# Fused sparse attention and mixer: start-up order, transposes of the first batch, place of the strided work, and the last accumulation step

## The chip, the cores and the metric

The kernel runs on one core of a Trainium2 chip. The metric is the device time of one execution in microseconds (us): the median of three runs, and, for the analysis, one profiled execution with its trace.

The core has five engines with a queue each, worked off in order: TensorE (PE, with PEld for its weight loads), VectorE (DVE), ScalarE (ACT), GpSimd (POOL) and SyncE (SP). SP, ACT and POOL also start DMA transfers; a DMA that has to wait holds up what stands behind it in the same queue.

## The reference

There are 8 batches of 8 heads, 576 positions and head size 64. Heads 0 to 3 attend to the last 32 positions ("local"), heads 4 to 7 to the positions of the same residue modulo 32 ("strided"). The attention output, 576 x 512 for a batch, then goes through a mixer:

```
scores = q @ k.T / 8, masked (local or strided), softmax, @ v  -> x
h = x^T @ U @ V            (U: 576 x 32, V: 32 x 576)
u = x + h^T
out = u + relu(u @ w_ch1) @ w_ch2      (512 -> 2048 -> 512)
```

## The kernel before

**The blocks.** The two large products are made block by block. A block n has four row tiles of 128 positions of one batch; a ninth block holds the last 64 positions of all batches. A block has 16 steps fc: `gemm1` (12 matmuls, L668) makes 128 hidden columns, ACT and DVE split the result into a high and a low part `gh`, `gl` (L673, L674), and one step later `gemm2` (12 matmuls, L686) adds them into four accumulators, each 128 x 512 in PSUM, held in two tiles of two. `finish` (L693) adds the accumulators to x on DVE, one row tile after the other, and stores them. Operands are split in high and low parts because the fast number format is not exact; `split` (L659, L660) does this for u at the end of a block, from `raw`, which 32 small DMAs fill from transposed tiles `bt` (`transposes`).

**The start-up.** `first_attention` makes the attention of batches 0 and 1 in eight head pairs, four a batch, in the order strided, strided, local, local. The text calls them P1 to P8 in that order (P1 to P4 are batch 0). A pair loads k and q together (`load_qk`), then v (`load_v`); PE adds the mask into PSUM as a matmul with the bf16 identity `ident_b` (L338) and then the scores (L357); DVE takes maximum and difference (L367, L368), ACT the exponential (L372); PE transposes the result with the f32 identity `ident` (L379), ACT copies it out (L382), PE multiplies by v (L397), DVE divides (L408 to L415). For batch 0 `quarter` follows: it transposes the pair's part of x with `x_transposed` (L312, a matmul with `ident`), multiplies by U (L286, L288), adds the product with V on top of the transposed x (L295), and splits the sum into a quarter of `uh`, `ul`. The first step of block 0 needs all four quarters. Idle stretches of PE ahead of P1's and P2's scores are filled with `WARM` matmuls on zeros (L336), eight each. The three constants (strided mask, local mask with `ident_b`, and `ident`) are loaded on POOL's queue; everything else comes on SP's queue. `small_weights` converts U (L129 to L132, two copies L144, L145) and then V, in separate steps of the start-up.

**The weights** come as 64-bit words. They are loaded on SP in 23 units and converted on ACT and DVE (L129, L131, L132, L205, L206) during block 0, up to four steps ahead of their use. The buffer `early` also lies in the place of the first large unit.

**The rest of the attention.** In block n the attention of batch n+1 is made in small steps that `advance` hands out by slot (two slots a step, 32 a block): `A_EARLY`, `A_LATE`, `A_TAIL` say from which slot to which slot how many steps. From batch 2 on, the strided heads are made without PE in `strided_heads`: POOL multiplies (L467 scores, L495 values), DVE sums (L445, through `reduced`, which puts a sum behind the last `finish` traced before it). `S0` and `S1` say in which slots, `N_STRIDED` how many steps; for batch 2 it starts in slot 16 of block 0, and its steps run from slot 22 to slot 12 of block 1. When the attention reaches the mark "strided", what is left of the strided steps is issued at once, and then `strided_copies` (L512, L516) moves the result into x on ACT, followed by `mix_t`, `mix_u`, `mix_tail` and `transposes`.

**What sets the order.** The program is traced in the order of the code, and a list scheduler with a time model then fixes each engine's order; `tc.issue_after` adds an edge. So a slot is a priority and, through buffers and edges, sometimes a bound; it is no fixed time.

## Time and profile before

| | us |
|---|---|
| median of three runs | 918.03 |
| lowest, highest | 916.94, 919.47 |
| the profiled execution, its own time | 918.08 |
| span of its trace, first to last instruction | 916.0 |
| PE busy / DVE busy / POOL busy / ACT busy in the span | 893.4 / 548.3 / 339.4 / 253.2 |

The profiled execution is 0.05 us from the median, so sums made on its trace can be compared with the median directly. Busy times have to be read stage by stage: the share of PE in the span is a mean over a start-up, nine blocks and a tail, and an engine with a low share can still be the one that a stage waits for.

### The profile page before, as it was taken

To read this page: it belongs to the slowest core of one execution; us is meant where nothing else is said; L and a number is where in the kernel's file an instruction comes from. 1 tells how busy PE (TensorE), PEld (TensorE's weight loads), DVE (VectorE), ACT (ScalarE), POOL (GpSimd) and SP (SyncE) were. 2 spreads that over 40 slices of the span, in tenths; PEclk is the share of its full clock that TensorE was granted. 3 is DMA by queue.
4 is the path that set the end of the run, shared out by engine and by line. 5 is a ranking of instruction groups with operands and counts; after the bars stand their busy time and mean duration, and the time that the engine had idled before them with its cause. 6 is when DMAs were issued, how large, how long until landed. Compare 5 with 4: busy or idle time off the path is not lost.

```text
span 916.0 us, 16587 instructions
## 1 busy us (share of the span) xinstructions
PE 893.4 (98%) x6862; PEld 714.1 (78%) x6862; DVE 548.3 (60%) x899; ACT 253.2 (28%) x501; POOL 339.4 (37%) x378
## 2 busy tenths in 40 slices
PE   7899989999999999999999999999999999999997
PEld 4677768887888787878887888878787888888885
DVE  4678997856786588738873877477754331122111
ACT  3456422241224122521242123312241211121110
POOL 1232484636563475429450946175620000000000
PEclk9899999999999999999999999999999999999999
DMA  9869313210331015011401050103200230001001
GB/s 355 308 211 357 118 44 116 72 53 3 86 135 42 12 52 183 1 53 31 165 28 53 21 187 28 53 9 124 91 1 3 57 116 23 1 1 47 0 1 47
DMA packets 30843, 75.27 MB, mean 82 GB/s; under 512 B 6464, under 2 KB 14672, under 8 KB 28848
## 3 DMA queue, kind: packets, MB, share of 16 engines
q1 hardware_dynamic: 29360, 71.07, 22.6%
q0 software_dynamic: 1088, 2.62, 0.9%
q8 instruction: 54, 0.88, 0.4%
q10 hardware_dynamic: 320, 0.52, 0.2%
q14 instruction: 21, 0.17, 0.1%
HBM read 54.14 MB, written 11.67 MB: 72 GB/s over the span
## 4 chain that ended last, share of the span: by engine, by line
PE 84%; DVE 4%; DMA 2%; POOL 1%; issue 1%; ACT 1%; SPq 0%; DVEq 0%; POOLq 0%; ACTq 0%
PE acc L686 40%; PE ph L668 39%; PE px L397 1%; DMA w<-in_w_dram 1%; PE px L357 1%; PE px L379 1%; DVE s_st L445 1%; PE px L536 1%; PE px L558 1%; DVE cv L132 1%; DMA st<-in_strided_dram 1%; DVE w L206 1%; DMA od<-x 1%; DVE gl L674 0%; POOL tmp L467 0%
## 5 line engine op out<-in xcount | busy, mean ns | idle before, releaser
L674 DVE SCALAR_TENSOR_TENSOR gl<-ph,gh 128x512 fp32r<-128x512 f32 x144 | 98.5, 685 | 233.7 <-ACT gh L673 232.9
L467 POOL TENSOR_TENSOR tmp<-st 128x576 f32<-128x576 f32 (+6 forms) x162 | 177.0, 1128 | 127.6 <-DMA st<-in_strided_dram 71.7
L668 PE MATMUL ph<-uh,w 128*128 128x512 f32 x648 | 215.4, 391 | 0.0
L673 ACT ACTIVATE gh<-ph 128x512 fp32r<-128x512 f32 x144 | 85.7, 597 | 449.0 <-PE ph L668 424.8
L686 PE MATMUL acc<-w,gh 128*128 128x512 f32 x648 | 196.3, 391 | 0.0
L495 POOL TENSOR_TENSOR tmp<-st,s_st 128x448 f32<-128x448 f32 (+7 forms) x162 | 137.0, 876 | 128.2 <-DVE st L445 51.2
L686 PEld LDWEIGHTS acc<-w,gh 128*128 128x128 f32 x648 | 121.2, 188 | 26.8 <-issue 1.2
L668 PEld LDWEIGHTS ph<-uh,w 128*128 128x128 f32 x648 | 121.7, 188 | 26.0
L445 DVE TENSOR_REDUCE st<-tmp 128x64 f32<-128x64 f32 (+8 forms) x162 | 135.6, 882 | 2.6 <-POOL tmp L495 2.1
L668 PE MATMUL ph<-ul,w 128*128 128x512 f32 x324 | 126.4, 390 | 0.0
L686 PE MATMUL acc<-w,gl 128*128 128x512 f32 x324 | 121.8, 391 | 4.2 <-DVE gl L674 4.2
L445 DVE TENSOR_REDUCE s_st<-tmp 128x9 f32<-128x576 f32 (+6 forms) x162 | 86.4, 561 | 14.0 <-POOL tmp L467 13.4
L686 PEld LDWEIGHTS acc<-w,gl 128*128 128x128 f32 x324 | 60.8, 188 | 18.7 <-DVE gl L674 5.9
L668 PEld LDWEIGHTS ph<-ul,w 128*128 128x128 f32 x324 | 60.8, 188 | 12.5
L512 ACT COPY xg<-st 32x256 f32<-32x256 f32 x96 | 38.8, 404 | 10.7 <-DVE st L445 9.0
L660 DVE TENSOR_TENSOR ul<-raw,uh 128x256 fp32r<-128x256 f32 x64 | 25.4, 432 | 12.9 <-ACT uh L659 12.5
L693 DVE TENSOR_TENSOR xg<-acc,xg 128x512 f32<-128x512 f32 x36 | 22.7, 682 | 17.4 <-PE acc L686 17.4
L659 ACT CAST uh<-raw 128x256 fp32r<-128x256 f32 x64 | 23.2, 404 | 19.5 <-DMA raw<-bt 10.2
L668 PE MATMUL ph<-uh,w0a 128*128 128x512 f32 x72 | 24.1, 391 | 0.0
L668 PE MATMUL ph<-uh,w1a 128*128 128x512 f32 x72 | 23.9, 391 | 0.0
L668 PE MATMUL ph<-uh,w2a 128*128 128x512 f32 x72 | 23.9, 391 | 0.0
L668 PE MATMUL ph<-uh,w6a 128*128 128x512 f32 x72 | 23.8, 392 | 0.0
(266 smaller groups left out, 1231.6 us busy)
## 6 DMA issues: line engine op xcount, KB each, us to landing
w<-in_w_dram SPq DMA_DIRECT2D x9, 1024.0 KB, 13.3
raw<-bt SPq DMA_DIRECT2D x256, 32.0 KB, 1.8
out_dram<-xg SPq DMA_DIRECT2D x32, 256.0 KB, 5.2
v<-in_pairs_dram SPq DMA_DIRECT2D x12, 585.0 KB, 5.1
st<-in_strided_dram SPq DMA_DIRECT2D x6, 1152.0 KB, 5.5
qk<-in_pairs_dram SPq DMA_DIRECT2D x12, 576.0 KB, 6.1
late<-in_pairs_dram SPq DMA_DIRECT2D x8, 585.0 KB, 8.2
late<-in_pairs_dram SPq DMA_DIRECT2D x8, 576.0 KB, 8.1
```

The lines of the kernel that those rows point to most:

```text
L132: nc.vector.scalar_tensor_tensor(out=i, in0=lo_w, scalar=29, in1=i, op0=ALU.logical_shift_right, op1=ALU.bitwise_or)
L445: nc.vector.tensor_reduce(**what)
L467: nc.gpsimd.tensor_tensor(out=tmp[:, 0:n], in0=sk[:, j0:j0 + n], in1=sq[:, i:i + 1].broadcast_to([128, n, D]), op=ALU.mult)
L495: nc.gpsimd.tensor_tensor(out=tv, in0=sv[:, 0:i + 1, d0:d0 + step], in1=s_st[:, i, 0:i + 1].broadcast_to([128, i + 1, step]), op=ALU.mult)
L512: nc.scalar.copy(out=xg[32 * i4:32 * i4 + 32, :, cs], in_=o_st[rows, i4:16:4, :])
L659: nc.scalar.copy(out=hi, in_=raw[:, t, :, :, dc, :])
L660: nc.vector.tensor_tensor(out=lo, in0=raw[:, t, :, :, dc, :], in1=hi.bitcast(F32), op=ALU.subtract)
L668: last = nc.tensor.matmul(ph, w_parts[fc, 0][:, part, 128 * dc:128 * dc + 128], ut[:, dc, :], start=(dc == dcs[0] and i == 0), stop=(dc == ...
L673: marks.setdefault("gh", []).append(nc.scalar.activation(out=gh, in_=ph, func=AF.Relu).ins)
L674: low = nc.vector.scalar_tensor_tensor(out=gl, in0=ph, scalar=0.0, in1=gh.bitcast(F32), op0=ALU.max, op1=ALU.subtract)
L686: last = nc.tensor.matmul(accs[n][s // 2][:, s % 2, :], gt[:, cs], w_parts[fc, 1][:, part, :], start=(fc == 0 and i == 0 and n > 0), stop= ...
L693: last = nc.vector.tensor_tensor(out=ot, in0=accs[n][s // 2][:, s % 2, :], in1=ot, op=ALU.add)
```

## The change

**Start-up.** One DMA on SP, first in that queue, brings the strided mask and `ident_b` together (`mask_first`, in `early`). `ident` follows on SP behind the k and q of P1 and P2, the local mask behind the v of P1. POOL loads none of them. The second group of `WARM` matmuls falls from eight to three. U's conversion stands behind the second exponential, where it stood behind the first copy of transposed probabilities, and in one step with V's.

**Transposes.** `x_transposed` uses TensorE's transpose mode.

**Strided work and attention slots.** For batch 2 the strided work starts in slot 20 (its steps from slot 26) and ends by slot 20 of block 1. The value products go by residue of the chunk index modulo 4, and the ACT copies into x become steps of `strided_heads`, one group behind the sums. The attention steps of blocks 1 to 6 go in two paces, local pairs first and then the mix, with own slots for block 1.

**Last step.** In the last step of the last block the accumulators are completed tile by tile, in order, and the fourth lies in a tile of its own.

```diff
-N_LATE = 47
-N_STRIDED = 66
+N_LOCAL = 20
+N_REST = 16
+N_STRIDED = 74
...
-A_LATE = (2, 26, N_LATE)
+A_LATE = (3, 12, 26)
+A_SECOND = (1, 19, 27)
...
-S0 = {2: 16, **{b: 32 * (b - 1) - 12 for b in range(3, 8)}}
-S1 = (12, 12)
+S0 = {2: 20, **{b: 32 * (b - 1) - 12 for b in range(3, 8)}}
+S1 = (20, 12)
 ORDER0 = (2, 3, 0, 1)
-WARM = {0: 8, 1: 8}
+WARM = {0: 8, 1: 3}
...
-    masks_sb = const.tile([128, 448], BF16, name="masks_sb")
-    mask_l, ident_b = masks_sb[:, 0:320], masks_sb[:, 320:448]
+    mask_l = const.tile([128, 320], BF16, name="mask_l")
...
-    mask_s = early[:, 1600:1760].bitcast(BF16)
+    mask_first = early[:, 1600:1824].bitcast(BF16)
+    mask_s, ident_b = mask_first[:, 0:320], mask_first[:, 320:448]
...
-        with tc.issue_after(marks["PT"][0]), tc.issue_after(marks["less"][1]):
+        with tc.issue_after(marks["exp"][1]), tc.issue_after(marks["less"][1]):
             f = to_f32(words_in, early, 128, 10 * R)
         nc.scalar.copy(out=U_sb.rearrange("p t r -> p (t r)"), in_=f[:, 0:5 * R])
         nc.scalar.copy(out=late[0][:, 1816:1816 + 5 * R], in_=f[:, 5 * R:10 * R])
-        yield
...
                 return nc.tensor.matmul(pu[:, 128 * t:128 * t + n], part, ident[0:n, 0:n], start=t == 0, stop=False,
-                                        skip_group_check=True).ins
+                                        is_transpose=True, skip_group_check=True).ins
...
-        far_dma(out=mask_s, in_=masks[:, 448:768])
-        far_dma(out=masks_sb, in_=masks[:, 0:448])
-        far_dma(out=ident, in_=eye)
-        for first in (heads[0], heads[1], heads[0], heads[2], heads[1], sw, heads[3], heads[2], heads[3]):
+        dma(out=mask_first, in_=masks[:, 0:448])
+        for n, first in enumerate((heads[0], heads[1], heads[0], heads[2], heads[1], sw, heads[3], heads[2], heads[3])):
             next(first)
+            if n == 1:
+                dma(out=ident, in_=eye)
+            if n == 2:
+                dma(out=mask_l, in_=masks[:, 448:768])
...
-            if tick in (1, 2):
+            if tick == 2:
                 next(sw)
...
-            accs[n] = [ps_acc.tile([128, 2, 512], F32, name="acc") for _ in range(2)]
-        for s in range(4):
+            pair = [ps_acc.tile([128, 2, 512], F32, name="acc") for _ in range(2)]
+            accs[n] = [pair[s // 2][:, s % 2, :] for s in range(4)]
+            if n == B:
+                accs[n][3] = psx1()
+        for s in tiles:
...
-        if len(pend) > 1:
+        if len(pend) > 1 and step < len(steps) - 1:
             gemm2(*pend.pop(0))
...
-    while pend:
-        gemm2(*pend.pop(0))
+    gemm2(*pend[0])
+    for s in range(4):
+        with tc.issue_after(marks["acc"][-1]):
+            gemm2(*pend[1], (s,))
     finish(NB - 1)
```

In `strided_heads` the loop over the 18 chunks becomes a loop over the groups (16 and 17; 0, 4, 8, 12; 1, 5, 9, 13; 2, 6, 10, 14; 3, 7, 11, 15); when a group's sums have been traced, the four heads' ACT copies of the group before are traced, with a step after every second head. `strided_copies` is gone, and the attention goes from the mark "strided" to `mix_t`.

## Rows read from the trace of the kernel before

**Rows 1.** The page's first part: busy time of each engine, its share of the span and its instructions.
```profile
PE 893.4 (98%) x6862; PEld 714.1 (78%) x6862; DVE 548.3 (60%) x899; ACT 253.2 (28%) x501; POOL 339.4 (37%) x378
```

**Rows 2.** TensorE's matmuls in order of time in the start-up, merged: start, length, line, operands, count, and in brackets the idle time before and what ended it. The last row is P8's mask.
```profile
8.08 0.68 PE L338 MATMUL acc<-early,masks_sb 128*128 128x320 bf16 x2 [3.23 <-DMA masks_sb<-in_masks_dram]
8.69 1.31 PE L357 MATMUL acc<-late 64*32 64x32 f32 x72
9.94 2.69 PE L336 MATMUL px<-raw 128*128 128x512 bf16 x8
...
13.18 0.86 PE L379 MATMUL acc<-ident,late 128*128 128x128 f32 x5
...
18.94 1.52 PE L312 MATMUL acc<-ident,early 128*128 128x128 f32 x10
...
29.40 2.69 PE L312 MATMUL acc<-ident,early 128*128 128x128 f32 x10
...
34.64 1.24 PE L379 MATMUL acc<-ident,late 128*128 128x128 f32 x5
...
37.82 1.16 PE L312 MATMUL px<-ident,xg 128*128 128x128 f32 x8
...
43.66 1.13 PE L312 MATMUL acc<-ident,xg 128*128 128x128 f32 x8 [1.28 <-DVE xg L411]
...
48.75 0.50 PE L668 MATMUL ph<-uh,w0a 128*128 128x512 f32 x1
...
57.61 0.45 PE L338 MATMUL acc<-masks_sb 128*128 128x320 bf16 x2
```

**Rows 3.** DMA issues by line, with count, size and median us from issue to landing: P1's k and q (the first issue of the first us), P2's (the second), U, and the last stores on ACT's queue.
```profile
late<-in_pairs_dram SPq DMA_DIRECT2D x1, 576.0 KB, 4.1
...
late<-in_pairs_dram SPq DMA_DIRECT2D x1, 576.0 KB, 5.3
...
xg<-in_U_dram SPq DMA_DIRECT2D x1, 320.0 KB, 9.2
...
out_dram<-xg ACTq DMA_DIRECT2D x4, 128.0 KB, 3.4
```

**Rows 4.** SP's queue in order of time: start, length, what is issued, count.
```profile
0.74 2.59 SPq L96 DMA_DIRECT2D late<-in_pairs_dram  x5
3.38 0.49 SPq L96 DMA_DIRECT2D xg<-in_U_dram  x1
...
46.68 0.33 SPq L96 DMA_DIRECT2D w<-in_w_dram  x1
...
227.45 20.14 SPq L96 DMA_DIRECT2D raw<-bt  x32
```

**Rows 5.** Busy time of one slice of one us: start and end, length, busy us of PE, PEld, DVE, ACT, POOL with instruction counts, granted TensorE clock, DMA share, GB/s.
```profile
29.00:30.00 1.00, 1.00 (x33) 0.83 (x16) 0.49 (x1) 0.00 (x0) 0.00 (x0) 0.50 0.99 394
```

**Rows 6.** ScalarE in order of time: the first weight conversion, P3's copy of transposed probabilities, the first large unit's conversion, and the last casts of `split` for block 2.
```profile
19.95 0.67 ACT L129 ACTIVATE cv<-w0a 128x512 f32<-128x512 f32 x1 [0.60 <-DMA w0a<-in_w_dram]
...
24.96 0.63 ACT L382 COPY late<-px 128x576 f32<-128x576 f32 x1
...
77.98 1.15 ACT L129 ACTIVATE cv<-w 128x1024 f32<-128x1024 f32 x1
...
249.17 1.02 ACT L659 CAST uh<-raw 128x256 fp32r<-128x256 f32 x3 [0.62 <-DMA raw<-bt]
```

**Rows 7.** What TensorE waited for from 75 to 130 us and from 130 to 880 us (us in total, times, longest); the first row is of the first stretch, the second the largest of the second.
```profile
PE acc L686 <- DVE gl L674: 3.5, 3, 1.6
...
PE acc L686 <- DVE gl L674: 0.7, 1, 0.7
```

**Rows 8.** VectorE in order of time: one weight subtraction without and one beside POOL's products, and the seventeenth sum of batch 2's scores.
```profile
95.51 1.20 DVE L206 TENSOR_TENSOR w<-cv,w 128x1024 fp32r<-128x1024 f32 x1
...
111.76 2.34 DVE L206 TENSOR_TENSOR w<-cv,w 128x1024 fp32r<-128x1024 f32 x1
...
130.84 0.38 DVE L445 TENSOR_REDUCE s_st<-tmp 128x4 f32<-128x256 f32 x1
```

**Rows 9.** GpSimd in order of time: the gate of batch 2's strided load, and its value products.
```profile
99.52 0.40 POOL L452 COPY st<-w 1x1 f32<-1x1 f32 x1 [16.45 <-ACT w L205]
...
161.87 7.51 POOL L495 TENSOR_TENSOR tmp<-st,s_st 128x320 f32<-128x320 f32 x9 [9.22 <-DVE st L445]
...
187.83 2.29 POOL L495 TENSOR_TENSOR tmp<-st,s_st 128x576 f32<-128x576 f32 x2 [0.85 <-DVE st L445]
```

**Rows 10.** The page's costliest groups: busy us and mean ns of one, then idle time before and its releaser.
```profile
L467 POOL TENSOR_TENSOR tmp<-st 128x576 f32<-128x576 f32 (+6 forms) x162 | 177.0, 1128 | 127.6 <-DMA st<-in_strided_dram 71.7
```

**Rows 11.** The chain that ended last, in order of time, around the first mix of batch 2 and the start of block 2.
```profile
212.02 1.00 PE px L536 x8
...
247.56 5.44 PE acc L686 x24
253.00 5.44 PE ph L668 x24
```

**Rows 12.** All engines in order of time at the end.
```profile
908.68 2.48 DVE L693 TENSOR_TENSOR xg<-acc,xg 128x512 f32<-128x512 f32 x4 [3.21 <-PE acc L686]
...
909.16 0.39 PE L686 MATMUL acc<-w,gl 128*128 128x512 f32 x1
...
909.41 2.74 ACTq L99 DMA_DIRECT2D out_dram<-xg  x4
```

More of the change, by code (lines that the diff above doesn't have):

```diff
@@ new lines, in strided_heads @@
+        done = []
+        for i4 in (4, 0, 1, 2, 3, None):
+            for i in () if i4 is None else range(16, NCH) if i4 == 4 else range(i4, 16, 4):
+                step = D if i < 9 else D // 2
+                for d0 in range(0, D, step):
+                    tmp = att([128, (i + 1) * step], "tmp")
+                    tv = tmp.rearrange("p (j d) -> p j d", d=step)
+                    nc.gpsimd.tensor_tensor(out=tv, in0=sv[:, 0:i + 1, d0:d0 + step],
+                                            in1=s_st[:, i, 0:i + 1].broadcast_to([128, i + 1, step]), op=ALU.mult)
+                    late.append(lambda tv=tv, i=i, d0=d0, step=step: reduced(
+                        out=o_st[:, i, d0:d0 + step], in_=tv.rearrange("p j d -> p d j"), axis=AX.X, op=ALU.add))
+                    flush(1)
+                    yield
+            flush(0)
+            done.append(i4)
+            if len(done) == 1:
+                continue
+            i4 = done[-2]
+            assert len(marks["out"]) == b - 1
+            xg, xt = x_tiles(b)
+            for h in range(4):
+                rows = slice(32 * h, 32 * h + 32)
+                cs = slice(256 + D * h, 256 + D * h + D)
+                if i4 < 4:
+                    nc.scalar.copy(out=xg[32 * i4:32 * i4 + 32, :, cs], in_=o_st[rows, i4:16:4, :])
+                else:
+                    for x in range(2):
+                        nc.scalar.copy(out=xt[tb + 32 * x:tb + 32 * x + 32, cs], in_=o_st[rows, 16 + x, :])
+                if h % 2:
+                    yield
@@ L692, in finish @@
             ot = xgs[n][:, s, :]
[L693 removed]
+            last = nc.vector.tensor_tensor(out=ot, in0=accs[n][s], in1=ot, op=ALU.add)
             if n == B:
```

48 lines of the change are left out of this document (13 added, 35 removed).

## The prediction

> **What bounds the kernel now.** I read the busy times first, then PE in order of time, then what PE waits for. PE is busy 893.4 of 916.0 us [rows 1], so all idle time of PE together is 22.6 us, and only work taken off PE can bring more. The question is where these 22.6 us lie. Of the waits, the largest after the start-up are for `gl`, 3.5 us between 75 and 130 and 0.7 from there to 880 [rows 7]. At the end PE's last matmul ends at 909.16 + 0.39 = 909.55, and the span at 916.0, which is 6.4 us [rows 12]. The rest, some 12 us, lies in the main ahead of the first gemm, which starts at 48.75 [rows 2]. So blocks 0 to 8 are PE-bound, and a gain comes from an earlier first gemm, from the stalls of block 0, or from the tail. What the reader should see in the start-up: PE's first scores stand behind a wait of 3.23 us for a mask [rows 2], and part of it runs at a granted clock of 0.50, which is 1.2 of 2.4 GHz [rows 5].
>
> **The masks.** The first scores are released by `masks_sb` at 8.08, at 8.69 they start [rows 2]. P1's k and q have landed at 0.74 + 4.1 = 4.84 [rows 3, 4]. After the change the mask lies ahead of them in the same queue: one more issue of 2.59 / 5 = 0.52 us [rows 4]. So P1's scores start near 5.4 instead of 8.69, -3.2 us; the bounds are -3.9 (the extra issue hidden) and 0 (the landing in its new queue no earlier than now). `ident` and the local mask come behind the loads of P1 and P2; the transposes that need `ident` come after scores, maximum, difference and exponential, 13.18 - 8.69 = 4.5 us later than the scores [rows 2], and that covers it. Without that cover it would cost the 0.5 us of an issue. They delay every load behind them by up to three issues, 1.5 us, where the queue's issue and not the transfer is the limit.
>
> **The warm matmuls.** Eight take 2.69 us, 0.34 each, at mixed clock [rows 2]; five fewer are -1.7. P2's k and q, the second in the queue, are there at about 1.3 + 5.3 + 0.5 = 7.1 [rows 3, 4], and P1's scores and three warm matmuls end at 5.4 + 1.3 + 1.0 = 7.7, so P2's scores can use all of it. P1's own chain, through DVE and ACT to its transposition, doesn't pass the warm matmuls and wins nothing. Of two chains that alternate on the same engines I count one: -0.8, bounds -1.7 and 0.
>
> **The transposes of x.** L312 now shows 10 matmuls for five tiles, L379, a transposition, five for five [rows 2]. The four quarters cost 1.52, 2.69 (at half clock), 1.16 and 1.13; as transpositions 0.86, 1.24 (L379 at half clock), and four tiles of 0.86 / 5 twice, 0.69. That is -0.66, -1.45, -0.47, -0.44, in sum -3.0. The first three stand among work of PE without a pause before them, so most of this is on its path; before the last PE waits 1.28 for DVE, and the transposition follows in the chain itself [rows 2]. I take -2.2, bounds -3.0 and 0. The Trainium skill (TensorE: Matmul & The Clock Gate, Terms) calls the transpose mode 4 times faster for FP32: by that the four would cost a quarter, and the sum be -4.9. The rows give a factor of 1.6 to 2.2, and I go by the rows.
>
> **U's steps.** U lands at 3.38 + 9.2 = 12.6 [rows 3, 4], which doesn't move. If the first pair is 3 us earlier, U's conversion behind the first copy would stand in ACT's queue before its data are there, and behind it the second exponential; moved behind that exponential it meets data that have landed. The same instructions run, and P1's multiplication by U waits for them: 0, bounds -1 and +1.
>
> **What doesn't move.** The first weights land at 19.95 [rows 6], at the end of a row of loads; the DMA engines are still full at 29 us, with a share of 0.99 [rows 5]. ACT copies P3's transposed probabilities at 24.96 behind the conversions [rows 6]. If ACT keeps that order, the copy can't come earlier than 19.95 plus the conversion itself, two casts and two vector steps of 0.4 to 0.7, an estimate of 2.4 us from the first row's 0.67: 22.4, or -2.6 us. So of the 4.0 us from masks and warm matmuls, 1.4 can be lost here. I take +1.2, bounds 0 and +1.4.
>
> **Start-up, sum:** -3.2 - 0.8 - 2.2 + 1.2 = -5.0; bounds -8.6 and 0 (U's +1 or -1 aside). The pairs of batch 1 and the weight loads behind them start from the same work and move with it, so I take the shift through block 0 undiminished. `early` is now held until P8's mask is in PSUM, as `ident_b` lies in it, and the first large weight unit waits for that: its load was issued at 46.68 [rows 4], and its conversion starts at 77.98 [rows 6]. P8's mask stands at 57.61 [rows 2], so the load comes 11 us later in its stage; the 31 us to the conversion hide that, and without them it would be up to 11.
>
> **Strided work of batch 2.** The stalls in block 0 are waits for `gl`, which stands in DVE's queue behind weight conversions and sums. POOL's products make these dearer: the same subtraction takes 1.20 us before and 2.34 beside them [rows 8]. But the strided load is held by a gate, the conversion of a weight unit, until 99.52 [rows 9], not by its slot 16, so slot 20 changes little at the start. What changes is the bound behind: with steps from slot 26 to 52 only 73 x 6 / 26 = 16 to 17 of 27 score sums are traced before block 0's `finish`, and the rest must wait for it. The seventeenth now ends at 131.2 [rows 8], so DVE is freed from there, and POOL's products stop somewhat before. Of 3.5 + 0.7 us [rows 7] I take -2, bounds -4.2 and +2 (if the order made from the model puts more sums ahead of `gl`).
>
> **The price of that in block 1.** The values begin at 161.87 behind `finish` and end at 190.1 [rows 9]; the mix starts at 212.02 [rows 11]. After: eleven scores of 1.13 [rows 10] behind `finish` take 12.4 us, the load of v and the softmax an estimate of 7 (the rows' loads take 4.1 in a free and 9.2 in a full queue [rows 3]), and 27 products at the old pace (28.2 us for the last 23) 33: 161.9 + 12.4 + 7 + 33 = 214. That is just the mix's time. Behind it 32 copies take 20.14 us of SP's queue [rows 4], the last casts wait for them until 250.2 [rows 6], and PE needs them at 253.0 [rows 11]. So 2.8 us are spare: 0, bounds 0 and +4. ACT's copies of x now stand among the sums; a sum that is late holds `gh` behind them, but `gh` has the time of a whole gemm, 5.44 / 2 = 2.72 us [rows 11], to spare, so 0. In the later blocks PE waits hardly at all, 0.7 us for `gl` [rows 7], so the new paces can bring no more.
>
> **The tail.** Four additions on DVE take 2.48 us from 908.68 to 911.16 [rows 12], 0.62 each, though only the last needs PE's last matmul at 909.55. Tile by tile the last one ends at 909.55 + 0.65 = 910.2: -0.9. The stores behind it, issue and 3.4 us landing [rows 3], stay. Bounds -0.5 and -1.3.
>
> **Sum.** -5.0 - 2.0 + 0 - 0.9 = -7.9, from 918.08 to 910.2; the profiled execution is 0.05 us from the median.
>
> **The rivals.**
> Gain lost in the start-up: the chain of ACT and DVE or the DMA queue sets the first gemm, and of 5.0 us only 1 to 2 arrive. For it: the DMA engines are full [rows 5], and the weights' landing doesn't move. Against it: PE's own work shrinks too. Time: 918.1 - 1.5 - 0.9 - 0.5 = 915.2.
> Clock: part of the start-up already runs at 0.50 [rows 5], and with fewer warm matmuls and lighter transpositions the slow stretch may last longer. L312's ten took 2.69 us there against 1.52, a factor of 1.77 [rows 2]; 8 us more at that clock hold work of 4.5, which is +3.5: 913.7. The Trainium skill (TensorE: Matmul & The Clock Gate, Part 4: PE-mode transpose) says that the full clock doesn't engage for the transpose mode, which speaks for this rival; the trace neither shows nor excludes it, as L379's transpositions are too short.
> Clock, the other way: an early start without the pause before 8.08 keeps the full clock, the start-up gains its bound and block 0 its stalls: 918.1 - 8.6 - 3.5 - 0.9 = 905.
> Slower: batch 2's strided work ends too late for block 2. Each us of the mix beyond 212 + 2.8 is one of PE. To outweigh the gain of 7.9 the mix has to start after 223, which takes products 30% slower than estimated; at 226, 11 us are lost: 921.
> The transposition changing nothing (mode not taken) would be 912.4, within the forecast's range.
>
> **How the numbers follow.** Chances: forecast (906.5 to 913.5) 0.58, gain lost 0.15, slow clock 0.10, gain beyond 0.10, slower 0.07. A measurement can tell about 0.3%, 2.8 us, from no change: faster means below 915.3, slower above 920.8. Faster: 0.58 + 0.10 + 0.10 and 0.05 of the lost gain, 0.83; slower 0.07; the same 0.10. The range from 905.0 to 916.0 holds all but the slower case and a small part of the ends.
>
> **What would show it.** In the profile after: P1's scores near 5.4 and no wait for a mask; five matmuls a quarter at L312 near 0.17 us each; the first gemm near 44; stalls on `gl` between 100 and 140 of about 2 us; no wait of PE at the start of block 2; the last addition ending 0.65 us after the last matmul. It is wrong if the first gemm starts after 47, if PE pauses between 240 and 260, or if the first gemm is early and block 0 ends no earlier.

## The result and the profile after

The changed kernel takes 924.74 us (median of 5 runs, 923.01 to 927.49); the kernel before took 916.94 beside it (5 runs, 916.15 to 919.47). The ratio is 1.0086, with a 95% interval from 1.0058 to 1.0113: about 8 us slower, where 7.9 us faster had been forecast.

Busy time tells nothing of it. This is the first part of the page after, which answers to [rows 1]: TensorE has 0.8 us less work than before, and the span is 7 us longer, so TensorE's idle time has grown by 7.8.

```profile
span 923.0 us, 16535 instructions
...
PE 892.6 (97%) x6838; PEld 711.2 (77%) x6839; DVE 547.8 (59%) x899; ACT 253.1 (27%) x501; POOL 334.0 (36%) x375
```

Milestones show where. The start of block 0's first gemm, the sixteenth `gh` of each block and the end of the last matmul, in both traces (us):

| | before | after | difference |
|---|---|---|---|
| first gemm of block 0 | 48.75 | 47.31 | -1.44 |
| last `gh` of block 0 | 151.39 | 149.78 | -1.61 |
| last `gh` of block 1 | 247.66 | 246.10 | -1.56 |
| last `gh` of block 2 | 343.90 | 345.07 | +1.17 |
| last `gh` of block 3 | 440.78 | 444.94 | +4.16 |
| last `gh` of block 4 | 537.03 | 542.53 | +5.50 |
| last `gh` of block 5 | 633.88 | 640.18 | +6.30 |
| last `gh` of blocks 6, 7, 8 | 730.07, 817.11, 904.15 | 737.73, 824.77, 911.81 | +7.66 |
| end of the last matmul | 909.55 | 917.21 | +7.66 |
| end of the span | 915.97 | 922.97 | +6.99 |

So the start-up brought 1.4 us, block 0's stalls 0.2, the tail 0.7; blocks 2 to 6 lost 9.2; blocks 7 and 8, which have no strided work beside them, lost nothing. What TensorE waited for from 140 to 740 us in the kernel after (in total, times, longest) names `gh`, `gl` and `ul`, the three that stand at the start of a block:

```profile
PE acc L693 <- ACT gh L677: 2.9, 2, 2.3
PE acc L693 <- DVE gl L678: 2.4, 3, 0.9
PE ph L672 <- DVE ul L664: 1.3, 2, 1.0
PE ph L672 <- ACT uh L663: 0.3, 1, 0.3
```

The longest wait is at the start of block 3. TensorE there, in order of time, in the kernel after (the first two rows are the block's first matmuls, of two different steps):

```profile
350.25 0.39 PE L672 MATMUL ph<-uh,w0a 128*128 128x512 f32 x1
350.48 0.39 PE L672 MATMUL ph<-uh,w1a 128*128 128x512 f32 x1
...
358.76 1.21 PE L693 MATMUL acc<-w0b,gh 128*128 128x512 f32 x4 [2.26 <-ACT gh L677]
```

DVE at the same place:

```profile
350.75 2.00 DVE L664 TENSOR_TENSOR ul<-raw,uh 128x256 fp32r<-128x256 f32 x3
352.67 1.27 DVE L700 TENSOR_TENSOR xg<-acc,xg 128x512 f32<-128x512 f32 x2
353.87 1.25 DVE L664 TENSOR_TENSOR ul<-raw,uh 128x256 fp32r<-128x256 f32 x1
355.04 4.39 DVE L446 TENSOR_REDUCE st<-tmp 128x32 f32<-128x544 f32 x5
359.35 0.67 DVE L678 SCALAR_TENSOR_TENSOR gl<-ph,gh 128x512 fp32r<-128x512 f32 x1
```

And ACT:

```profile
357.21 1.01 ACT L518 COPY xt<-st 32x64 f32<-32x64 f32 x4 [7.48 <-DVE st L446]
358.13 1.06 ACT L677 ACTIVATE gh<-ph 128x512 fp32r<-128x512 f32 x2
```

The last view first: two `gh` run back to back at 358.13, so both products had been waiting; ahead of them four copies of the strided result stand in ACT's queue; ACT stands idle for 7.48 us ahead of them, until a sum of DVE ends; and on DVE the same sums stand ahead of `gl`, which starts at the moment at which the fifth ends.

In blocks 4 to 6 TensorE waits for `gl` instead. Block 4 in the kernel after, first TensorE, then DVE:

```profile
450.12 0.39 PE L672 MATMUL ph<-uh,w0a 128*128 128x512 f32 x1
...
457.71 0.50 PE L693 MATMUL acc<-w0b,gl 128*128 128x512 f32 x1 [0.76 <-DVE gl L678]
```

```profile
451.81 5.24 DVE L446 TENSOR_REDUCE st<-tmp 128x32 f32<-128x544 f32 x6
456.98 0.68 DVE L678 SCALAR_TENSOR_TENSOR gl<-ph,gh 128x512 fp32r<-128x512 f32 x1
```

And the same place in the kernel before, where TensorE doesn't wait:

```profile
445.96 0.39 PE L668 MATMUL ph<-uh,w0a 128*128 128x512 f32 x1
```

```profile
447.66 3.71 DVE L445 TENSOR_REDUCE st<-tmp 128x64 f32<-128x64 f32 x7
451.29 0.68 DVE L674 SCALAR_TENSOR_TENSOR gl<-ph,gh 128x512 fp32r<-128x512 f32 x1
```

Two suspects, then: the copies on ACT, or the sums on DVE. The experiments separate them.

TensorE in the start-up of the kernel after, in order of time, which answers to [rows 2]:

```profile
5.36 1.11 PE L358 MATMUL acc<-late 64*32 64x32 f32 x72
...
17.81 1.38 PE L313 MATMUL acc<-ident,early 128*128 128x128 f32 x5 [0.46 <-DVE early L412]
...
24.35 0.50 PE L296 MATMUL acc<-xt,tst 96*128 96x512 f32 x1 [1.78 <-DVE tst L294]
...
28.07 1.41 PE L313 MATMUL acc<-ident,early 128*128 128x128 f32 x5
...
35.41 0.66 PE L313 MATMUL px<-ident,xg 128*128 128x128 f32 x4
```

ACT in the same stretch, which answers to [rows 6]:

```profile
20.07 0.67 ACT L131 ACTIVATE cv<-w0a 128x512 f32<-128x512 f32 x1 [1.33 <-DMA w0a<-in_w_dram]
...
23.16 0.25 ACT L292 CAST tst<-ph 32x128 fp32r<-32x128 f32 x1
```

And DVE's last additions, which answer to [rows 12]:

```profile
915.89 1.89 DVE L700 TENSOR_TENSOR xg<-acc,xg 128x512 f32<-128x512 f32 x3 [2.76 <-PE acc L693]
917.69 0.68 DVE L700 TENSOR_TENSOR xg<-px,xg 128x512 f32<-128x512 f32 x1
```

P1's scores start 3.3 us earlier, and the first transposition 1.1 us earlier. But the product with V starts at 24.35, where it started at 24.29 before: there the gain is gone. It waits for `tst`, and `tst` stands on ACT behind the conversion of `w0a`, which waits for its weights. The kernel before, TensorE and then ACT:

```profile
24.29 0.50 PE L295 MATMUL acc<-xt,tst 96*128 96x512 f32 x1
```

```profile
24.04 0.20 ACT L154 CAST xt<-Vst 96x8 fp32r<-96x8 f32 x1
```

There `tst` was ready earlier, and the casts of V into `xt`, which also stand behind the conversion, ended last, at 24.24.

### The profile page after: what moved, and what is told of

Its sections match the earlier page's. It is cut to its first block, busy times and chain, and to the rows that moved or that the text cites. A ratio compares the mean times of both kernels' runs of the same rounds, so it can differ in the third digit from the quotient of the medians.

```text
span 923.0 us, 16535 instructions
## 1 busy us (share of the span) xinstructions
PE 892.6 (97%) x6838; PEld 711.2 (77%) x6839; DVE 547.8 (59%) x899; ACT 253.1 (27%) x501; POOL 334.0 (36%) x375
## 4 chain that ended last, share of the span: by engine, by line
PE 85%; DVE 6%; issue 1%; ACT 0%; POOL 0%; DVEq 0%; POOLq 0%
PE acc L693 40%; PE ph L672 38%; DVE st L446 2%; DVE xg L700 1%; PE px L398 1%; PE px L693 1%; PE px L358 1%; PE px L380 1%; PE px L539 1%; PE px L561 1%; DVE ul L664 0%; DVE s_st L446 0%; DVE w L207 0%; DVE gl L678 0%; PE px L543 0%
## 5 line engine op out<-in xcount | busy, mean ns | idle before, releaser
L468 POOL TENSOR_TENSOR tmp<-st 128x576 f32<-128x576 f32 (+6 forms) x162 | 174.2, 1114 | 159.2 <-DVE s_st L446 66.6
L693 PE MATMUL acc<-w,gh 128*128 128x512 f32 x630 | 190.5, 390 | 0.0
L498 POOL TENSOR_TENSOR tmp<-st,s_st 128x576 f32<-128x576 f32 (+7 forms) x162 | 137.6, 874 | 101.0 <-DVE st L446 35.2
L693 PEld LDWEIGHTS acc<-w,gh 128*128 128x128 f32 x630 | 118.3, 188 | 25.1 <-issue 0.2
L446 DVE TENSOR_REDUCE st<-tmp 128x32 f32<-128x544 f32 (+8 forms) x162 | 134.2, 878 | 4.9 <-POOL tmp L498 4.7
L693 PE MATMUL acc<-w,gl 128*128 128x512 f32 x315 | 118.4, 390 | 2.9 <-DVE gl L678 2.9
L446 DVE TENSOR_REDUCE s_st<-tmp 128x9 f32<-128x576 f32 (+6 forms) x162 | 86.7, 561 | 10.4 <-POOL tmp L468 9.8
L700 DVE TENSOR_TENSOR xg<-acc,xg 128x512 f32<-128x512 f32 x35 | 22.1, 683 | 22.4 <-PE acc L693 22.4
L549 DVE TENSOR_TENSOR ta<-px,ta 32x512 f32<-32x512 f32 x21 | 14.4, 687 | 26.1 <-ACT ta L547 25.6
L693 PE MATMUL acc<-w0b,gh 128*128 128x512 f32 x70 | 21.4, 400 | 2.9 <-ACT gh L677 2.9
```

What stands on the lines that cost most here:

```text
L446: nc.vector.tensor_reduce(**what)
L468: nc.gpsimd.tensor_tensor(out=tmp[:, 0:n], in0=sk[:, j0:j0 + n], in1=sq[:, i:i + 1].broadcast_to([128, n, D]), op=ALU.mult)
L498: nc.gpsimd.tensor_tensor(out=tv, in0=sv[:, 0:i + 1, d0:d0 + step], in1=s_st[:, i, 0:i + 1].broadcast_to([128, i + 1, step]), op=ALU.mult)
L549: nc.vector.tensor_tensor(out=ta, in0=ps_a[32 * j:32 * j + 32, :], in1=ta, op=ALU.add)
L693: last = nc.tensor.matmul(accs[n][s], gt[:, cs], w_parts[fc, 1][:, part, :], start=(fc == 0 and i == 0 and n > 0), stop=(fc == NFC - 1 and ...
L700: last = nc.vector.tensor_tensor(out=ot, in0=accs[n][s], in1=ot, op=ALU.add)
```

## Experiments

All ratios are to the kernel before, timed beside each run. Block times are last `gh` to last `gh`. "Sums ahead" are value sums (L446) that DVE starts between the last `gl` of the block before and the first `gl` of the block, with their durations added up. Diffs show the lines that matter; `...` marks what is left out.

### First round: four parts

**Copies behind all sums.**
```diff
-            if len(done) == 1:
-                continue
-            i4 = done[-2]
+        for i4 in done[:-1]:
```


> The changed kernel with one thing undone: ACT's copies of the strided result stand behind all sums of DVE again; the order of the groups, the slots and paces, the start-up and the tail stay as changed. First theory (the copies among the sums hold gh and so gl, and PE waits at the starts of blocks 1 to 6): the 9.2 us lost between the last gh of block 1 and the last of block 6 shrink to 0 to 3, the total is 915.5 to 918.5, and L518's wait for a sum is below 2 us. Rival (the later slots and new paces move the work into the next block): the copies are as late as before or later, the loss stays at 8 to 10, the total at 924 to 926.

935.86 us, ratio 1.0210 (1.0189 to 1.0230). Neither theory had this. The list scheduler didn't follow the place in the code: the copies of chunks 16 and 17, whose sums are still the first, stand ahead of the first `gh` as before, six in block 2 and four in blocks 3 to 6. The edit undid nothing, so it speaks for neither theory. The sums ahead take 4.7 to 5.6 us, and the first `gl` starts 7.1 to 9.6 us after the block's first matmul, where it starts 6.8 to 9.1 after it in the changed kernel. One more reason why it costs twice as much shows in slices of two us around its longest wait (columns as in [rows 5]): in an idle of 3.05 us of TensorE, up to 262.47, the granted clock falls to 0.50, 1.2 GHz, and stays there for some 7 us.

```profile
260.00:262.00 2.00, 0.00 (x0) 0.00 (x0) 2.00 (x4) 0.76 (x4) 2.00 (x4) 0.90 0.94 385
262.00:264.00 2.00, 1.53 (x4) 1.24 (x5) 1.55 (x3) 1.50 (x4) 2.00 (x4) 0.50 0.22 88
264.00:266.00 2.00, 2.00 (x6) 1.57 (x5) 2.00 (x4) 0.00 (x0) 1.32 (x3) 0.50 0.04 8
```

**Slots and paces of before.**
```diff
-A_LATE = (3, 12, 26)
-A_SECOND = (1, 19, 27)
+A_LATE = (2, 26, 35)
...
-S0 = {2: 20, ...}
-S1 = (20, 12)
+S0 = {2: 16, ...}
+S1 = (12, 12)
...
+            a0, a1, total = A_EARLY if n == 0 else A_LATE if n + 1 < B else A_TAIL
...
```


> The changed kernel with the slots and paces of the kernel before for the strided load and for the attention of blocks 1 to 7; the copies still stand among the sums. First theory (order in ACT's queue): PE still waits for gh and gl at the starts of the blocks, the loss there stays at 6 to 10 us, the total is 921 to 926. Rival (slots and paces): the loss is 0 to 2, the total 915 to 917.

936.97 us, 1.0223 (1.0196 to 1.0250). The rival falls: with the old slots the loss doesn't go, it grows (16.6 us over blocks 2 to 6). The first theory's direction holds, its size (6 to 10) doesn't.

**The start-up alone**, on the kernel before (masks, identity, U's steps, `WARM` 3, transpose mode).
```diff
-WARM = {0: 8, 1: 8}
+WARM = {0: 8, 1: 3}
...
+        dma(out=mask_first, in_=masks[:, 0:448])
...
+                                        is_transpose=True, skip_group_check=True).ins
...
```


> The kernel before with the parts of the start-up alone: masks, order of the identity's load, three warm matmuls, U's steps behind the second exponential, transposition mode. Strided work, slots and tail as before. If the start-up really brings no more than 1.4 to 1.6 us: the first gemm near 47.3, the total 1.0 to 2.0 below the kernel before, no loss at the starts of the blocks. By the prediction on record: the first gemm near 44, the total 5.0 below. If the start-up has a hand in the loss of the later blocks: above the kernel before.

918.22 us, 1.0005 (0.9988 to 1.0023): no change that can be measured. In its trace the first gemm is 0.3 us earlier, block 0 ends 0.8 later, and blocks 2 to 6 take what they took before. The start-up has no hand in their loss; and its forecast of -5.0 is wrong.

**The transpose mode alone.**
```diff
-                                        skip_group_check=True).ins
+                                        is_transpose=True, skip_group_check=True).ins
```


> The kernel before with the transposition mode alone. By the prediction on record: the four quarters 0.86, 1.24, 0.69 and 0.69, the first gemm 2.2 earlier (46.5), the total 2.2 lower. First rival, PE's work is covered by ACT's chain: the quarters shrink, but the first gemm moves by less than 0.5 and the total by less than 0.5. Second rival, the clock: the stretch at a granted clock of 0.50 grows by more than 3 us, and the first gemm is not earlier or is later.

919.07 us, 1.0017 (0.9999 to 1.0035). The step itself is right: the four quarters take 0.86, 0.86, 0.66 and 0.66, and the first gemm starts 2.07 earlier (forecast 2.2). But in the same execution block 0 gives it back behind one wait for instructions (`issue`: nothing that the profile shows ends it; the last section says why it is read so), in which the granted clock also falls to 0.50 (54 to 61 us):

```profile
46.68 0.50 PE L668 MATMUL ph<-uh,w0a 128*128 128x512 f32 x1
...
56.35 0.44 PE L397 MATMUL acc<-late 64*32 64x65 f32 x7 [4.46 <-issue]
```

That execution was the slowest of its ten (916.47 to 923.43), so its 4.46 is an extreme, but the median has no gain either. That the transposition mode keeps the clock low, one half of the clock rival, falls here: the granted clock is 1.00 from 10 to 50 us, through all four quarters. The other half, the warm matmuls, comes in the third round.

### Second round: copies or sums

**Copies held behind `gh`** by an added edge.
```diff
+                    with tc.issue_after(marks["gh"][-1]):
                         nc.scalar.copy(out=xg[32 * i4:32 * i4 + 32, :, cs], ...)
```


> The changed kernel, with an added edge: each ACT copy of the strided result stands behind the last gh traced before it. By the order that this gives, no copy stands ahead of a block's first gh (blocks 2 to 6), where the changed kernel has four; on DVE the four half sums of chunks 16 and 17, and up to three more, still stand ahead of the first gl. Theory A (the copies in ACT's queue hold gh): the loss between the last gh of block 1 and the last of block 6, 9.2 us in the changed kernel, falls to 0 to 2, total 915 to 918. Theory B (the wide sums in DVE's queue hold gl, with or without the copies): PE waits for gl in place of gh, the loss stays at 6 to 12, total 922 to 928.

930.36 us, 1.0131 (1.0103 to 1.0159). No copy stands ahead of a first `gh`, and blocks 4 to 6 take 97.6 to 97.7 us, as with the copies there: theory A falls. The total lies above theory B's range too, since block 2 alone takes 107.0, behind a wait of 2.7 for `uh` and one of 2.5 for `gl`: with its copies held back, batch 2's mix starts at 217.94 and not at 214.02. TensorE's waits from 140 to 740 us are now for `gl` in the main:

```profile
PE acc L695 <- DVE gl L680: 6.9, 5, 2.5
PE ph L674 <- ACT uh L665: 2.7, 1, 2.7
PE acc L695 <- ACT gh L679: 0.3, 1, 0.3
```

**Chunks in order, copies behind them.**
```diff
-        for i4 in (4, 0, 1, 2, 3, None):
-            for i in () if i4 is None else range(16, NCH) if i4 == 4 else range(i4, 16, 4):
+        for i4 in (0,):
+            for i in range(NCH):
...
+        for i4 in range(5):
...
```


> The changed kernel with the value products of the strided heads in the order of the chunks, 0 to 17, as before, and the ACT copies traced behind them; slots, paces, start-up and tail as changed. By the order that this gives, ACT's first copy stands behind the block's third gh, and the sums ahead of the first gl are the seven narrowest, as in the kernel before. Theories A and B alike: the loss at the starts of the blocks is 0 to 1, total 915 to 917.5. Rival (the new slots and paces cost by themselves): the loss stays above 5, total above 921.

920.03 us, 1.0019 (1.0005 to 1.0034). Blocks 3 to 6 are back at 96.2 to 97.0; block 2 keeps 2.4 us, behind a wait of 1.6 for `ul`. So something else has a price of its own, in block 2 alone; the new slots are the suspect.

**Chunks 16 and 17 last**, copies still among the sums.
```diff
-        for i4 in (4, 0, 1, 2, 3, None):
+        for i4 in (0, 1, 2, 3, 4, None):
```


> The changed kernel with its groups in another order: residues 0, 1, 2, 3 and then chunks 16 and 17, with the copies still among the sums, one group behind. By the order that this gives, no copy stands ahead of a block's first gh, three or eight of the first groups behind the first or second one. If the order of the groups is what costs: loss 0 to 2, total 915 to 918.5. If copies among the sums cost wherever they stand in the first steps: loss 4 to 9, total 919 to 925.

931.77 us, 1.0147 (1.0121 to 1.0174). Worse than both cases that I had written down. No copy stands ahead, but six to seven sums do, of 4.2 to 5.1 us (the fourth chunk of the first group is already wide), and the waits are for `gl`, 5.7 us. These sums are no longer than in the changed kernel, but they start later. DVE in block 4, whose first matmul is at 453.09:

```profile
457.18 4.46 DVE L446 TENSOR_REDUCE st<-tmp 128x64 f32<-128x64 f32 x7
461.56 1.27 DVE L678 SCALAR_TENSOR_TENSOR gl<-ph,gh 128x512 fp32r<-128x512 f32 x2
```

They start 4.1 us after that matmul, behind `ul` and the additions of `finish`, where they start 1.7 after it in block 4 of the changed kernel (451.81 and 450.12).

**Eight warm matmuls** in the changed kernel.
```diff
-WARM = {0: 8, 1: 3}
+WARM = {0: 8, 1: 8}
```


> The changed kernel with eight warm matmuls ahead of the second pair in place of three. If the longer stretch at a granted clock of 0.50 (from about 13 to 23 us) comes from the missing warm matmuls: the clock is 1.00 again by 14, the first gemm at 45 to 46.5, total 1 to 2.3 below the changed kernel. If it comes from the pauses of PE behind them (waits for the exponential and for instructions): the same stretch at 0.50, the first gemm at 47 to 48.5, total within 1 of the changed kernel's.

927.69 us, 1.0094 (1.0062 to 1.0126). The clock now stays at 1.00 until 17, and the first transposition starts at 14.98. It brings nothing: `w0a` landed at 22.1 in this execution, and the product with V waits 5.51 for `tst`, until 26.35. The first gemm starts only at 53.89, outside both cases; this execution was the slowest of the four. Conversion and product lie 4.28 apart in the kernel after (20.07 and 24.35), 4.34 before (19.95 and 24.29), 4.29 with the chunks in order (20.92 and 25.21), 4.25 here (22.10 and 26.35) and 4.51 with the mode alone (19.74 and 24.25). So the product seems to move with the weights' landing; the next round tests it.

### Third round: no sums ahead, and the weights out of the way

**No value sum ahead of the first `gl`.**
```diff
-N_STRIDED = 74
+N_STRIDED = 60
...
+    def reduced_gl(**what):
+        with tc.issue_after(marks["gl"][-1]) if "out" in marks else nullcontext():
+            reduced(**what)
...
```


> The changed kernel with its groups in the order of the change, the wide chunks 16 and 17 first, and its copies among the sums, but with the value sums behind the last gl traced before each (an added edge) and a slower pace of the strided steps (60 for 74), so that the order has no value sum between the last gl of a block and the first gl of the next, where the changed kernel has three to six of 3.5 to 5.7 us. Theory B (DVE's sums ahead of the first gl are the loss): the blocks 3 to 6 take 96.2 to 96.9 us each, as before, in place of 97.6 to 99.9; the loss between the last gh of block 1 and the last of block 6 is 0 to 3 (block 2 may keep 2.4 from its own slots), total 915.5 to 918.5. Rival (the groups and the copies among the sums cost in whatever place, or the later sums hold the mix): blocks 3 to 6 at 97.5 or more, total above 921.

931.73 us, 1.0135 (1.0109 to 1.0162), and still theory B's blocks: 4 to 6 take 96.2, 96.9 and 96.2. Block 3 misses with 97.9, behind a wait of 1.5 for `uh`. The total misses too, since the slower pace, or the edge, made batch 2's result late: TensorE waits 11.3 us for `uh` ahead of block 2. That wait is the forecast's "slower" rival, provoked.

**The same from batch 3 on**, batch 2 at its own pace and without the edge.
```diff
+        with tc.issue_after(marks["gl"][-1]) if len(marks.get("out", ())) > 1 else nullcontext():
...
-        want = (N_STRIDED - 1) * (slot + 1 - s0) // max(1, s1 - s0)
+        want = (N_STRIDED - 1 - 14 * (sb > NSP)) * (slot + 1 - s0) // max(1, s1 - s0)
```


> The changed kernel with its groups and copies as changed, but from batch 3 on the value sums behind the last gl traced before each and at the slower pace (60 for 74), so that no value sum stands between the last gl of a block and the first gl of the next in blocks 2 to 6; batch 2 at the changed kernel's pace. Theory B (sums ahead of the first gl are the loss): blocks 4 to 6 at 96.2 to 96.9 us, block 3 up to 98, block 2 at 96.2 to 99; total 915 to 919. Rival (the wide groups or the copies among the sums cost elsewhere): blocks 4 to 6 at 97.5 or more, total above 921.

920.31 us, 1.0029 (1.0013 to 1.0045). Blocks 3 to 6 take 96.85, 96.22, 96.85 and 96.16, within 0.03 of the kernel before, with the groups as changed; as the copies follow their sums, none of them stands ahead of a first `gh` either. The total is 1.3 above the range that theory B gave, and 4.4 us below the changed kernel's: in the two traces blocks 2 to 6 take 6.9 us less, but block 0 ends 1.9 later. The start of block 3 on DVE, in order of time: `gl` is first, and it waits for nothing of DVE's own.

```profile
353.55 1.28 DVE L704 TENSOR_TENSOR xg<-acc,xg 128x512 f32<-128x512 f32 x2
357.73 0.69 DVE L682 SCALAR_TENSOR_TENSOR gl<-ph,gh 128x512 fp32r<-128x512 f32 x1 [2.90 <-ACT gh L681]
358.34 2.19 DVE L446 TENSOR_REDUCE st<-tmp 128x32 f32<-128x544 f32 x2
```

**Chunks in order and old slots together.**
```diff
+        for i4 in (0,):
+            for i in range(NCH):
...
+A_LATE = (2, 26, 35)
...
+S1 = (12, 12)
...
```


> The changed kernel with the value products in the order of the chunks, the copies behind them, and the slots and paces of the kernel before. If the 2.4 us that block 2 lost in the run with the order of the chunks alone come from the new slots of batch 2 (its result late for block 2): no wait for ul at the start of block 2, block 2 at 96.2 to 96.9, total 915.5 to 918. If they come from something else: the wait of 1.6 for ul stays, total 919 to 921.

920.92 us, 1.0026 (1.0016 to 1.0037): by its total the second case, by its waits the first. At the start of block 2 the wait for `ul` is gone; the block takes 97.6 (it was 98.7), behind a late `gl`, which starts 6.9 us after the block's first matmul. Block 1 loses 1.1 of its own, with a wait for batch 1's `ul` at its start. TensorE at the starts of blocks 1 and 2:

```profile
156.35 0.50 PE L668 MATMUL ph<-ul,w0a 128*128 128x512 f32 x1 [0.66 <-DVE ul L660]
...
262.18 0.50 PE L689 MATMUL acc<-w0b,gl 128*128 128x512 f32 x1 [0.52 <-DVE gl L674]
```

So the wait for `ul` ahead of block 2 belongs to the new slots; the old ones, with the other paces as changed, cost about as much elsewhere.

**`w0a` converted behind the first `tst`**, on the kernel before with the start-up and the tail of the change; with three and with eight warm matmuls.
```diff
-            with tc.issue_after(behind[0]), tc.issue_after(behind[1]):
+            with tc.issue_after(behind[0]), tc.issue_after(behind[1]), tc.issue_after(marks["tst"][0]) if i == 0 else nullcontext():
...
```


> The kernel before with the start-up and the tail of the change, strided work and slots as before, and one added edge: the conversion of the first weight unit w0a stands behind the copies of the first quarter's product with U (tst) on ACT. Theory (ACT's conversion of w0a, which waits for its weights until 20 to 22 us, holds tst and with it the product with V, which came 4.25 to 4.34 us after that landing in every run so far): the product with V starts at 22 to 23 in place of 24.3, the first gemm at 45.5 to 47, the total 1.5 to 3.5 below the kernel before. Rival (PE at a granted clock of 0.50 or its waits for instructions set the pace): the product with V at 24 or later, the first gemm after 47.3, the total within 1 of the kernel before.

> As the run with the conversion of w0a behind tst, with eight warm matmuls ahead of the second pair in place of three. If the clock in that stretch is worth something once the weights no longer hold tst: full clock until the first transposes of x at about 15, the product with V at 21 to 22, the first gemm at 44.5 to 46, the total 2.5 to 4.5 below the kernel before. If not, as the run with three warm matmuls or up to 1 us later.

With three: 918.78 us, 0.9998 (0.9984 to 1.0012), no gain; the product with V at 23.08, just outside what was expected, but the first gemm at 49.66. With eight: 915.65 us, 0.9973 (0.9962 to 0.9985), the first version that beats both kernels. The product with V comes at 21.83; the first gemm only at 48.18, 2.2 later than expected, since the last quarter waits 2.23 for its `tst`, at 46.71, which stands behind a step in the conversion of another weight unit:

```profile
21.83 0.80 PE L294 MATMUL acc<-xt,tst 96*128 96x512 f32 x1 [1.66 <-DVE tst L292]
...
46.71 0.50 PE L294 MATMUL acc<-Vst,tst 96*128 96x512 f32 x1 [2.23 <-DVE tst L292]
...
48.18 0.50 PE L669 MATMUL ph<-uh,w0a 128*128 128x512 f32 x1
```

The two versions differ in the five warm matmuls alone, and the medians by 3.1 us (the intervals touch). In the traces the first gemm lies 1.5 apart, and the version with three waits 2.1 for instructions at P7's product with v, the one with eight not at all.

**Four units behind the `tst` of their quarter**, with that start-up and eight warm matmuls, and without the new masks (masks, identity and U as before; there the units also stand behind the casts of V).
```diff
...
+ tc.issue_after(marks["tst"][i]) if i < 4 else nullcontext()
...
```


> The kernel before with the start-up and the tail of the change, eight warm matmuls, and the conversions of the first four weight units each behind the tst of its quarter. If conversions in ACT's queue hold tst in all quarters: the wait of 2.2 for the last tst falls below 1, the first gemm at 45.5 to 47.3, the total 2.5 to 4.5 below the kernel before. If the conversions only move the wait (to the first weights or to the second step of block 0): the first gemm at 48 or a wait for w0a to w3a behind it, the total 1.5 to 2.8 below, as with the first unit alone.

> The kernel before with the transposition mode, the tail and the same four edges (and the first unit behind the casts of V), but with masks, identity and U's steps as before and eight warm matmuls. If the masks' earlier landing is worth nothing because the weights' landing and U's set the first product with V: first gemm and total within 1 us of the run with masks. If the masks carry the gain: the first gemm 1.5 us or more later than in that run, total 0 to 1.5 below the kernel before.

With the masks: 915.76 us, 0.9975 (0.9962 to 0.9988); the last wait for `tst` falls to 0.66 as in the first case, but the first gemm starts at 47.62, just behind what it gave, and the total is that of the run before. Without the masks: 918.22 us, 1.0000 (0.9983 to 1.0016), the first gemm at 48.57, neither case in full. The masks' early landing seems to bring some 2 us once the conversions don't stand in front of it. This is likely and not certain: the two intervals overlap, the versions also differ in U's steps and in one edge, and in the traces only 0.9 of it lies at the first gemm.

## Why the prediction was wrong

The total lies above the forecast range, and two of its own signs of being wrong appear: the first gemm starts after 47 (47.31), and TensorE pauses between 240 and 260 (0.27, 0.99 and 0.62 us). The terms, against the traces (us; the sum of the last column is +6.9, the span moved by +6.99):

| term | predicted | measured |
|---|---|---|
| start-up | -5.0 | -1.4 |
| stalls of block 0 | -2.0 | -0.2 |
| price in block 1 (seen in block 2) | 0 (0 to +4) | +2.4 |
| copies and sums at the starts of blocks 2 to 6 | 0 | +6.8 |
| tail | -0.9 | -0.7 |

The 6.8 and the 2.4 are the 9.2 of blocks 2 to 6, split by the runs with the chunks in order and without sums ahead, which keep 2.4 each in block 2. The blocks' times, and in brackets how long after the block's first matmul the first `gl` starts:

| block | before | after | copies behind `gh` | wide last | chunks in order | no sums ahead from batch 3 |
|---|---|---|---|---|---|---|
| 3 | 96.88 (6.1) | 99.87 (9.1) | 97.68 (6.9) | 100.96 (8.5) | 96.95 (6.2) | 96.85 (5.9) |
| 4 | 96.25 (5.3) | 97.59 (6.9) | 97.63 (6.9) | 99.20 (8.5) | 96.23 (5.2) | 96.22 (5.2) |
| 5 | 96.85 (5.9) | 97.65 (6.8) | 97.67 (6.9) | 98.96 (8.2) | 96.28 (5.2) | 96.85 (5.9) |
| 6 | 96.19 (5.3) | 97.55 (6.9) | 97.57 (6.9) | 97.99 (7.3) | 96.79 (6.1) | 96.16 (5.2) |
| sums ahead | 4.0 | 4.7 to 5.7 | 5.6 to 5.7 | 4.9 to 5.1 | 4.0 to 5.0 | 0 |
| copies ahead | 0 | 4 | 0 | 0 | 0 | 0 |

**The step that failed** is this one: "a sum that is late holds `gh` behind them, but `gh` has the time of a whole gemm, 5.44 / 2 = 2.72 us [rows 11], to spare, so 0." It holds inside the blocks of the changed kernel and not at their starts: all of TensorE's waits from 140 to 740 us lie at the starts. There TensorE interleaves the first gemms of two steps, so that two products are done together (the two `gh` at 358.13), and what follows is `gemm2` of the first, which needs `gh` and `gl` at once. And the step looked at `gh` alone, while `gl` on DVE is what comes last. Sums wait for `finish`, so they come free on DVE just ahead of the first `gl`. The kernel before puts its seven narrowest there, 4.0 us, and waits 0 to 0.3. The change puts the widest there: 4.7 to 5.7 us cost 0.8 to 3.0 a block.

What the block takes follows the start of its first `gl`, in whatever order the work stands: with 5.2 to 5.3 us after the first matmul it takes 96.2 to 96.3, with 6.9 97.6, with 8.2 99.0, with 9.1 99.9, so a us of delay costs about one us of the block. The one value off that line, 100.96, has a stretch of 3.4 us at a granted clock of 0.50 behind its wait. Blocks 3 to 6 of the first two experiments lie on the line as well, from 7.1 us and 97.9 to 9.1 and 99.9, but for two with such a stretch. That the sums delay `gl`, and not the copies, is shown twice: without copies ahead blocks 4 to 6 keep loss and `gl` (second and third column), and without sums ahead both go back. Length is one half of it, the start of the sums the other: 4.9 to 5.1 us cost more with the wide chunks last than 5.7 in the changed kernel, since they start 2.7 to 4.1 us after the first matmul and not 0.5 to 1.7 after it. In block 3 of the changed kernel they start 4.8 after it, behind the last `ul`. TensorE waits for `gh` there, behind the copies; but `gl` starts right when the sums end, and the matmul that needs it comes 1.3 us behind the first one of `gemm2`, after a wait of 0.11 for it. So without the copies it would have waited for `gl` just as long. That is read from the trace; no run isolates block 3. The run with the copies behind `gh` is 2.2 us shorter there, but its sums also start at 0.5 and not at 4.8.

**The price in block 1.** The mix was forecast for 214, and starts at 214.02. That is luck. The products of the values end at 207.1, since the work ahead of them starts 1.6 earlier, and scores, softmax and products take 5 us less than estimated. Behind them come the last sums and ACT's copies, until 210.4, and the mix only at 214; for these the sum had nothing. The step that failed is the next, that 2.8 us were spare: block 1 itself ends 1.6 earlier, so the mix came 3.6 later against it. SP's copies of `raw` in the kernel after:

```profile
229.75 20.17 SPq L98 DMA_DIRECT2D raw<-bt  x32
```

ACT's last casts for block 2:

```profile
251.26 1.32 ACT L663 CAST uh<-raw 128x256 fp32r<-128x256 f32 x4 [3.69 <-DMA raw<-bt]
```

TensorE at the first gemm of block 2:

```profile
253.44 0.50 PE L672 MATMUL ph<-ul,w0a 128*128 128x512 f32 x1 [0.99 <-DVE ul L664]
```

They end 2.3 later than [rows 4], and the casts start 2.1 later than [rows 6]. The run with the chunks in order and the old slots bears this out: there the mix starts 35.5 us ahead of the last `gh` of block 1, as before (35.7; in the changed kernel 32.1), and the wait for `ul` is gone. The forecast's rival "slower" has the sign of the result and this mechanism, but only 2.4 us of the loss.

**The start-up.** P1's scores came at 5.36 (forecast 5.4), the transpositions as forecast where the clock was full. The rival "gain lost in the start-up" came true: 1.4 of 5.0 us arrived. "What doesn't move" had the right place and too small a size: it let at most 1.4 us be lost behind the landing of `w0a`, by way of P3's copy. What stands behind that conversion is V's casts and `tst`, and with them P1's whole chain: at the product with V all of the 4.0 us from masks and warm matmuls are gone, and the 1.4 left is what came behind it.

The conversion is only part of it. Held behind `tst`, it lets the product come 1.3 us earlier (23.08 for 24.35), and eight warm matmuls then bring 1.2 more (21.83). So the term of -0.8 for five warm matmuls fewer failed too: with three, the granted clock is 0.50 from 13 to 23 us in the changed kernel, through P1's transposition (1.38 us in place of 0.86), and the medians of the two runs that differ in them alone lie 3.1 us apart, the run with eight ahead (likely, as their intervals touch). In the changed kernel itself, with the weights in the way, eight warm matmuls change nothing that the intervals can tell (1.0094 and 1.0086). In the other traces with this start-up and three warm matmuls the first gemm moves by -1.2 to 0 (+0.9 with `w0a` held back). With the weights out of the way and eight warm matmuls the total gains 2.7 (915.65), but not the 5.0; what holds the first gemm at 47.6 to 48.2 then stays open. A granted clock of 0.50 from 18 to 31 in the run of 915.65 is one candidate; no run isolates it.

**Stalls of block 0.** The waits for `gl` fell from 4.2 to 2.9, but a wait of 2.6 for instructions (0.5 before) and one of 2.0 for `xt` (1.2 before) took their place: the term was right in kind, and its gain of 1.3 didn't arrive. The tail's last addition ends 1.16 after the last matmul, forecast 0.65.

The Trainium skill (TensorE: Matmul & The Clock Gate, Terms) gives a factor of 4 for the transpose mode; the first quarter fell from 1.52 to 0.86 at full clock, 1.8. The Trainium skill (TensorE: Matmul & The Clock Gate, Part 4: PE-mode transpose) says that the full clock doesn't engage in that mode. The run with the mode alone doesn't bear it out: the granted clock is 1.00 from 10 to 50 us, through all four quarters. They stand among ordinary matmuls there, and no run has a longer stretch of transpositions alone.

## What to carry to other kernels

A slack read in the steady state of a block doesn't hold at its start: look there for what an in-order queue has just been allowed to issue, put its shortest work ahead of the critical instruction, and read when that instruction starts, not only how much work stands ahead of it. A list scheduler with a time model follows its model and not the place in the code, so read the order that came out before calling an experiment an undoing. And before adding up gains of a start-up, find what else stands in the queue that the last product waits for; here a conversion for later work, which waited for its load, stood there and took 1.3 of the 4.0 us that had been gained ahead of it.

## What the runs showed of the hardware

In an idle of 3.05 us of TensorE at the start of block 2 (copies behind all sums) the granted clock fell to 0.50 for some 7 us; in the idle of 2.26 at the start of block 3 in the changed kernel it stayed at 1.00; and just behind a wait of only 1.55 (wide chunks last, until 361.42) it fell too, for 3.4. So the length of one idle alone doesn't tell. TensorE's waits for instructions at the same matmuls (P7's product with v) came to 0.5, 2.0, 2.6 and 4.5 us in different traces, and to nothing in three; that is as large as the gains that were sought. The profile names no releaser for these waits. That they are for instructions is read from the DMA packets: in each of the fourteen traces that have such a wait, a packet of 16 KB on the instruction queue starts 2.2 to 2.8 us before TensorE goes on (53.86 and 56.35 with the mode alone).
